# Moving the attention stretches and mixes of batch 1 within FFN block 0, and one stretch of batch 7

## The chip, the cores and the metric

The kernel runs on one core of a Trainium2 chip. The metric is the device time of one execution in microseconds (us). The kernel before takes 837.13 us (median of 3 runs, 836.72 to 837.36).

## The reference

```python
kv = einsum('bhsd,bhse->bhde', k, v)              # 8 batches, 8 heads, 576 rows, 64 columns
out = einsum('bhsd,bhde->bhse', q, kv)
x = out / sqrt(mean(out*out, -1) + 1e-6) * g      # heads side by side: 576 rows of 512
u = x + (x^T @ U @ V)^T                           # U: 576x32, V: 32x576, mixes the rows
y = u + relu(u @ w_ch1) @ w_ch2                   # 512 -> 2048 -> 512
```

Everything is float32; the two weight matrices of the FFN are the large part.

## The kernel before

**Blocks of rows.** The 8 x 576 = 4608 rows of u are cut into nine blocks of 512. Blocks 0 to 2 go through the FFN directly. Blocks 3 to 8 go through it in three stages of two blocks each by a seven-product scheme (P1 to P7), in which one product with a piece of the weights is a unit. Every float32 factor is split into a high and a low float32r part, and a product is three matmuls (high-high, high-low, low-high).

**Block 0.** The FFN runs over 16 chunks f of 128 hidden columns. Chunks 0 to 4 of block 0 are interleaved by hand with the attention of batch 0. From chunk 5 on the loop in `build` runs: two halves of the first product (`ffn1`, six matmuls each), the relu in a high and a low part, two halves of the second product (`ffn2`) of the chunk before. So a chunk has four places behind which other work can be put, numbered 4f to 4f+3: behind the first half of `ffn1`, behind the relu, behind the first half of `ffn2` and behind the second. One such FFN step is six matmuls. Only in block 0 the weights, which arrive as 64-bit words, are also decoded: `decode_w` gives six VectorE and three ScalarE instructions a chunk, issued two chunks ahead (`AHEAD`), and from chunk 10 on a store of the decoded weights on SP's queue (`wf`). Behind each relu GpSimd stores quarters of finished weights (`SPREAD`, `weight_quarters`).

**Attention of the later batches.** Each batch has four pairs of heads. `RUNS` lists (pair, (block or stage, place)). At such a place `run(before, now, after)` issues one stretch for three pairs at once: on TensorE the t-product of the pair before (`t_product`, L387 and L390, x^T U), the kv product of the pair after (`kv_product`, L300) and the out product of the pair now (`out_product`, L319); then, on the other engines, `t4_step` (L400 to L406) splits the t-product into `t4`, `kv_move` (L181) copies kv, `squares` (L329 raw copies, L333 squares), `stats_step` (L348 to L351 and L343 to L345) and `mul_step` (L363) scale x, and `turn_step` (L377) turns it and sends it through DRAM to `ut32` (four stores, L380, and one load, L382). The stretch also starts the next kv and q loads. `MIXES` lists the places of `mix_step`: two matmuls `t4` x V (L463), two additions to `ut32` (L470), and for batch 1 a split into the high and low rows (L422, L423) that the next block's first product reads. The stages' places are numbered by units; there a mix comes in two parts (`mix_part`).

**Order.** TensorE's order is the program order, written by hand. The orders of VectorE, ScalarE and SP's queue come from the scheduler, which prefers what stands earlier in the program among what it holds ready; each engine then runs its list in order.

**Buffers.** `bank()` gives one of two accumulator banks (`pp`); a stretch takes both and so does a mix of a batch up to 2. x has two buffers (`x_sb`), the turned x (`xt`) one, `t4` three, `kv_sb` and `q_sb` one each.

```python
def run(before, now, after):
    one, two = banks()
    if before: t_product(*before, two[:, NT * D:NT * D + P])
    ...
    if now: out_product(*now, (one, two))
    if before: t4_step(*before)
```

Of the kernel before, what the change touches and what calls it, by code (L numbers as in the profile page):

```python
# [37 lines left out]
KEEP = 4  # L38
FROM_DRAM = 5
COMBOS = [(1, f) for f in (1, 2, 4, 5, 7, 8, 10, 11, 13, 14)] + [(2, f) for f in (4, 5, 7, 8, 10, 11)]  # L40
RUNS = [((1, 0), (0, 20)), ((1, 1), (0, 28)), ((1, 2), (0, 37)), ((1, 3), (0, 45)), ((2, 0), (0, 54)),
# [4 lines left out]
MIXES = {(1, 0): ((0, 26),), (1, 1): ((0, 43),), (1, 2): ((0, 51),), (1, 3): ((0, 60),),  # L46
# [46 lines left out]
def build(ctx: ExitStack, tc: tile.TileContext, kv_in, kvt0_in, kvt_in, q_in, uv_in, g_in, w_in, out):  # L93
# [277 lines left out]
    def turn_step(b, p):  # L371

        x = state[b, p]["x"]
        xt = state[b, p].get("xt")
        if xt is None:
            xt = sc.tile([P, 4, NT, 32], F32, name="xt")
        nc.vector.transpose(out=xt.rearrange("p k i j -> p i k j"), in_=x.rearrange("p i (k j) -> p i k j", j=32))  # L377
        xd = xds[p % 2]
        for a in range(4):
            nc.sync.dma_start(out=xd[:, QO[a]:QO[a] + QL[a]].rearrange("(k j) n -> j k n", k=4),  # L380
                              in_=xt[32 * a:32 * a + 32, :, 0:QL[a] // 32].rearrange("p k i j -> p k (i j)"))
        nc.sync.dma_start(out=ut32[p], in_=xd)  # L382
# [154 lines left out]
    def x32_tiles(q):  # L537

        return [once(("x32", q % 2, i), lambda: const.tile([P, 2, 2 * BLK], F32, name="x32", tag=f"u_{2 - 2 * (q % 2) + i}"))
                for i in range(2)]  # L540
# [18 lines left out]
    def factor(q, names, es=slice(0, 2)):  # L559

        x11, x12, x21, x22 = [t[:, es, n * BLK:(n + 1) * BLK] for t in x32_tiles(q) for n in range(2)]
        t = st[:, es]

        def diff(a, b, t=t):
            less(t, a, b)
            return t

        plans = dict(P1=lambda: x11, P3=lambda: x22, P2=lambda: x21, P5=lambda: diff(x12, x11),
                     P6=lambda: diff(x22, t), P4=lambda: diff(x21, t), P7=lambda: diff(x22, x12, kept_t(2)[:, es]))
        for name in names.split():  # L570
            src = plans[name]()
            own = place(name)
            hi, lo = own[:, es, 0], own[:, es, 1]
            nc.scalar.mul(out=hi, in_=src, mul=g_sb)
            nc.vector.scalar_tensor_tensor(out=lo, in0=src, scalar=g_sb, in1=hi.bitcast(F32), op0=ALU.mult, op1=ALU.subtract)  # L575
# [485 lines left out]
    def run(before, now, after):  # L1061

        one, two = banks()
        if before:
            t_product(*before, two[:, NT * D:NT * D + P])
        if after:
            kv = (two if after[0] < NATIVE and after[1] % 2 else one)[:, BLK - D:]
            kv_product(*after, kv)
        if now:
            out_product(*now, (one, two))  # L1070
        if before:
            t4_step(*before)
        if after:
            kv_move(*after, kv)
            following(load_kv, *after)
        if now:
            squares(*now)
            stats_step(*now)
            mul_step(*now)
            following(load_q, *now)  # L1080
            if now not in TURNS:
                turn_step(*now)
# [16 lines left out]
    def at_block(n, what, j=NC - 1):  # L1099
        later.setdefault((None, j, n), []).append(what)  # L1100

    def at(spot, what):
        if spot[0] < NC:
            at_block(spot[1], what, spot[0])
        else:
            at_stage(spot[0] - NC, spot[1], what)
# [3 lines left out]
                         for i, t in enumerate(x32_tiles(0))])  # L1110
    pairs = [pair for pair, _ in RUNS]
    at(RUNS[0][1], lambda: run((1, 0), None, (1, 1)))
    for i, (pair, spot) in enumerate(RUNS[1:], 1):
        at(spot, lambda i=i, pair=pair: run(pairs[i - 1] if i > 1 else None, pair, pairs[i + 1] if i + 2 < len(pairs) else None))
    for pair, spot in TURNS.items():
        at(spot, lambda pair=pair: turn_step(*pair))
    for pair, spots in MIXES.items():
        if pair[0] > 2:
# [4 lines left out]
    for e, pair in enumerate((2, 3)):  # L1123
        at_block(MIXES[4, pair][1][1] + 1, lambda e=e: factor(0, "P1 P5 P6 P4 P2 P7 P3", slice(e, e + 1)))
    for b, spot in CARRY.items():
# [136 lines left out]
```

## Time and profile before

| | |
|---|---|
| median of 3 runs | 837.13 us (836.72 to 837.36) |
| the profiled execution | 837.33 us, of which 835.6 us are the profile's span |
| TensorE matmuls | 820.7 us, 98% of the span |
| TensorE weight loads | 673.2 us, 81% |
| VectorE / ScalarE / GpSimd | 585.4 us (70%) / 443.4 us (53%) / 80.3 us (10%) |
| DMA | 198.39 MB, mean 237 GB/s |

Busy times of matmuls overlap the weight loads (PEld). The timeline lists instructions with their start, duration, engine, line, output and inputs, and in brackets the idle time of the engine ahead of them and what ended it; the duration of a matmul is longer than the distance to the next, since they are pipelined. Times run from the start of the span. Block 0's loop from chunk 6 on lies between 64.79 and 138.58 us, the second Strassen-like stage begins at 517.97 us.

### The profile page before, as it was taken

The numbers are of one execution on the slowest core, as the hardware profiler recorded it, in microseconds if no ns is written. First come the engines' busy times: TensorE is split into PE (matmuls) and PEld (weight loads), VectorE is DVE, ScalarE is ACT, GpSimd is POOL, SyncE is SP. The second block draws the span as 40 slices with busy tenths as digits, with TensorE's granted clock in tenths as the row PEclk, the third lists the DMA queues.
The fourth block names the chain that finished last, engine by engine and source line by source line (L and its number), as shares of the span: only waits on it lengthen the run. The fifth ranks groups of instructions, "written<-read, shape, count | busy, mean of one in ns | idle before, by whom it ended". The sixth has DMA issues, their size and how long they took to land.

```text
span 835.6 us, 14368 instructions
## 1 busy us (share of the span) xinstructions
PE 820.7 (98%) x5492; PEld 673.2 (81%) x5492; DVE 585.4 (70%) x1016; ACT 443.4 (53%) x810; POOL 80.3 (10%) x159
## 2 busy tenths in 40 slices
PE   8999799999999999999999999999999999999998
PEld 7777678888888888888888888788888888888887
DVE  5999885888776678666785688568736943582376
ACT  5978752544443445365645664656346724542462
POOL 3002214244330221000000000000000000000000
PEclk9999999999999999999999999999999999999999
DMA  9984767699887779467777768667555685555554
GB/s 346 415 340 144 225 200 226 219 321 277 262 252 266 239 214 316 160 236 262 241 264 236 264 238 282 231 204 242 178 187 196 207 281 197 182 196 195 202 200 153
DMA packets 66357, 198.39 MB, mean 237 GB/s; under 512 B 8176, under 2 KB 27376, under 8 KB 55536
## 3 DMA queue, kind: packets, MB, share of 16 engines
q1 hardware_dynamic: 57184, 167.97, 58.9%
q0 software_dynamic: 8960, 29.37, 10.5%
q8 instruction: 43, 0.70, 0.3%
q14 instruction: 26, 0.21, 0.1%
q10 hardware_dynamic: 144, 0.13, 0.0%
HBM read 146.84 MB, written 50.59 MB: 236 GB/s over the span
## 4 chain that ended last, share of the span: by engine, by line
PE 83%; DVE 6%; DMA 6%; ACT 3%; issue 1%; SPq 0%; ACTq 0%; DVEq 0%
PE yy L671 25%; PE yy L773 23%; PE y L508 13%; PE h L484 5%; PE h L485 5%; PE h L486 4%; DMA w1raw<-w_in 2%; PE ya L723 2%; DMA out<-x 1%; DMA raw<-w_in 1%; PE pp L300 1%; PE pp L319 1%; DVE dec L164 1%; PE h L300 1%; DVE uc L575 1%
## 5 line engine op out<-in xcount | busy, mean ns | idle before, releaser
L671 PE MATMUL yy<-uc,wt 128*128 128x512 f32 x1008 | 234.1, 391 | 0.9 <-ACT t L405 0.9
L671 PEld LDWEIGHTS yy<-uc,wt 128*128 128x128 f32 x1008 | 188.0, 188 | 40.7 <-ACT t L405 1.3
L773 PE MATMUL yy<-dec,wt 128*128 128x512 f32 x468 | 113.8, 391 | 0.3 <-DVE dec L662 0.3
L508 PE MATMUL y<-hh,ws 128*128 128x512 f32 x336 | 113.4, 393 | 0.0
L773 PE MATMUL yy<-hh,wt 128*128 128x512 f32 x312 | 103.3, 390 | 0.0
L773 PEld LDWEIGHTS yy<-dec,wt 128*128 128x128 f32 x468 | 87.2, 188 | 18.9 <-DVE dec L662 0.7
L662 DVE TENSOR_TENSOR hl<-hk,hh 128x512 fp32r<-128x512 f32 x72 | 48.1, 686 | 39.7 <-ACT hh L701 39.5
L662 DVE TENSOR_TENSOR dec<-hk,dec 128x512 fp32r<-128x512 f32 x72 | 48.9, 686 | 37.1 <-ACT dec L701 36.7
L508 PEld LDWEIGHTS y<-hh,ws 128*128 128x128 f32 x336 | 63.1, 188 | 13.8
L773 PEld LDWEIGHTS yy<-hh,wt 128*128 128x128 f32 x312 | 58.6, 188 | 12.4
L484 PE MATMUL h<-ut,ws 128*128 128x512 f32 x168 | 67.5, 402 | 0.0
L485 PE MATMUL h<-ut,ws 128*128 128x512 f32 x168 | 66.6, 396 | 0.0
L486 PE MATMUL h<-ut,ws 128*128 128x512 f32 x168 | 66.4, 395 | 0.0
L508 PE MATMUL y<-hl,ws 128*128 128x512 f32 x168 | 65.8, 391 | 0.0
L773 PE MATMUL yy<-hl,wt 128*128 128x512 f32 x156 | 60.7, 389 | 0.0
L701 ACT CAST dec<-hk 128x512 fp32r<-128x512 f32 x72 | 44.2, 621 | 29.0 <-PE yy L773 14.9
L701 ACT CAST hh<-hk 128x512 fp32r<-128x512 f32 x72 | 44.0, 622 | 27.0 <-PE yy L773 22.8
L659 ACT COPY sp<-yy 128x1024 f32<-128x1024 f32 x35 | 35.5, 1014 | 32.6 <-PE yy L671 25.3
L496 ACT ACTIVATE hh<-h 128x512 fp32r<-128x512 f32 x48 | 28.4, 591 | 36.8 <-PE h L486 36.6
L684 ACT ACTIVATE hk<-hk 128x1024 f32<-128x1024 f32 x24 | 25.5, 1061 | 36.3 <-DVE hk L683 36.3
L659 ACT COPY yy<-yy 128x1024 f32<-128x1024 f32 x17 | 17.0, 998 | 43.4 <-PE yy L671 40.5
L501 DVE SCALAR_TENSOR_TENSOR hl<-h,hh 128x512 fp32r<-128x512 f32 x48 | 32.7, 682 | 9.4 <-ACT hh L496 9.4
(237 smaller groups left out, 1348.0 us busy)
## 6 DMA issues: line engine op xcount, KB each, us to landing
wt<-wd SPq DMA_DIRECT2D x84, 1024.0 KB, 4.9
kv_sb<-kv_in SPq DMA_DIRECT2D x29, 512.0 KB, 5.9
raw<-w_in SPq DMA_DIRECT2D x14, 1023.6 KB, 14.9
wd<-dec POOLq DMA_DIRECT2D x44, 256.0 KB, 5.7
wd<-ws POOLq DMA_DIRECT2D x42, 256.0 KB, 4.0
q_sb<-q_in SPq DMA_DIRECT2D x29, 288.0 KB, 6.3
ut<-xd SPq DMA_DIRECT2D x28, 288.0 KB, 4.1
out<-x SPq DMA_DIRECT2D x23, 256.0 KB, 4.6
```

The source lines that it names most:

```text
L484: nc.tensor.matmul(h, lhsT=w1s[f][0][:, d, :], rhs=uh[d], start=(n == 0), stop=False)
L485: nc.tensor.matmul(h, lhsT=w1s[f][0][:, d, :], rhs=ul[d], start=False, stop=False)
L486: nc.tensor.matmul(h, lhsT=w1s[f][1][:, d, :], rhs=uh[d], start=False, stop=(n == ND - 1))
L496: last["relu"] = nc.scalar.activation(out=last["hh"], in_=h, func=AF.Relu)
L501: last["low"] = nc.vector.scalar_tensor_tensor(out=hl, in0=h, scalar=0.0, in1=last["hh"].bitcast(F32), op0=ALU.max, op1=ALU.subtract)
L508: nc.tensor.matmul(acc, lhsT=w2s[f][w][:, c, :], rhs=h[:, cols], start=(f == 0 and w == 0 and h is hh), stop=(f == NF - 1 and w == 1))
L659: last["unit"] = nc.scalar.copy(out=pair_bank("P6") if name == "P1" else spare(name), in_=acc)
L662: return nc.vector.tensor_tensor(out=out, in0=a, in1=b, op=ALU.subtract)
L671: nc.tensor.matmul(acc[:, i], lhsT=w[:, ws_, e * P:(e + 1) * P], rhs=u[:, e, us], start=name in ("P1", "P5") and e == 0 and k == 0, stop=e ...
L684: last["unit"] = nc.scalar.activation(out=to, in_=to if other else acc, func=AF.Relu)
L701: last["unit"] = nc.scalar.copy(out=hh, in_=src)
L773: nc.tensor.matmul(acc[:, c], lhsT=w[:, ws_, c * P:(c + 1) * P], rhs=h, start=name in ("P1", "P5") and kk == 0 and i == 0, stop=kk == KEEP ...
```

## The change

Four places of `RUNS`, all four places of batch 1 in `MIXES`, and one more place of `RUNS` get other numbers; no other line differs.

```diff
-RUNS = [((1, 0), (0, 20)), ((1, 1), (0, 28)), ((1, 2), (0, 37)), ((1, 3), (0, 45)), ((2, 0), (0, 54)),
+RUNS = [((1, 0), (0, 20)), ((1, 1), (0, 25)), ((1, 2), (0, 33)), ((1, 3), (0, 41)), ((2, 0), (0, 50)),
...
-        ((6, 3), (3, 72)), ((7, 0), (3, 84)), ((7, 1), (4, 7)), ((7, 2), (4, 18)), ((7, 3), (4, 29)), (None, (4, 40))]
-MIXES = {(1, 0): ((0, 26),), (1, 1): ((0, 43),), (1, 2): ((0, 51),), (1, 3): ((0, 60),),
+        ((6, 3), (3, 72)), ((7, 0), (3, 84)), ((7, 1), (4, 7)), ((7, 2), (4, 20)), ((7, 3), (4, 29)), (None, (4, 40))]
+MIXES = {(1, 0): ((0, 30),), (1, 1): ((0, 45),), (1, 2): ((0, 54),), (1, 3): ((0, 61),),
```

The stretches of (1,1), (1,2), (1,3) and (2,0) in block 0 come three, four, four and four steps sooner; the mixes of (1,0) to (1,3) four, two, three and one step later. The `t4` of a pair is made in the stretch listed behind its own, so that of (1,1) in the stretch of (1,2). In the second of the three stages the stretch of (7,2), which makes the `t4` of (7,1), comes two units later; its mixes, at places 23 and 25, stay.

## Rows read from the trace of the kernel before

**Rows 1.** The page's head and its busy times by engine.

```profile
span 835.6 us, 14368 instructions
PE 820.7 (98%) x5492; PEld 673.2 (81%) x5492; DVE 585.4 (70%) x1016; ACT 443.4 (53%) x810; POOL 80.3 (10%) x159
```

**Rows 2.** TensorE's waits: line, what it waited for; us in total, times, longest.

```profile
PE pp L463 <- DVE t L406: 4.8, 2, 3.4
PE pp L387 <- DVE x L363: 1.2, 1, 1.2
...
PE yy L671 <- ACT t L405: 0.9, 1, 0.9
PE pp L300 <- DVE ut L470: 0.8, 1, 0.8
```

**Rows 3.** Windows: length, busy us (instructions) by engine, granted clock, DMA share, GB/s.

```profile
62.02:117.49 55.47, 50.12 (x388) 40.28 (x387) 48.16 (x85) 42.59 (x66) 9.98 (x16) 0.94 0.60 191
62.02:95.69 33.67, 31.74 (x256) 25.86 (x255) 31.20 (x55) 27.52 (x42) 7.62 (x12) 1.00 0.53 164
64.79:138.58 73.79, 67.04 (x526) 53.91 (x524) 58.47 (x110) 48.27 (x81) 18.41 (x31) 0.95 0.63 196
102.00:103.00 1.00, 1.00 (x4) 0.90 (x5) 1.00 (x4) 1.00 (x2) 1.00 (x2) 0.50 0.49 184
```

**Rows 4.** TensorE's timeline in block 0.

```profile
74.27 0.50 PE L484 MATMUL h<-ut,ws 128*128 128x512 f32 x1
...
89.88 0.50 PE L508 MATMUL y<-hh,ws 128*128 128x512 f32 x1
...
101.78 0.82 PE L463 MATMUL pp<-v,t 128*128 128x288 f32 x2 [3.42 <-DVE t L406]
102.39 0.63 PE L484 MATMUL h<-ut,ws 128*128 128x512 f32 x1
...
107.60 0.43 PE L387 MATMUL pp<-x,uf 128*32 128x128 f32 x8
...
109.53 0.50 PE L508 MATMUL y<-hh,ws 128*128 128x512 f32 x1
```

**Rows 5.** The chain that ended last, in block 0: start, us, what.

```profile
122.65 1.36 PE y L508 x6
...
130.28 2.72 PE y L508 x12
...
134.36 0.26 PE pp L463 x2
```

**Rows 6.** VectorE's timeline: the scaling of x by three stretches, one split.

```profile
87.00 0.82 DVE L363 TENSOR_TENSOR x<-x,half 128x640 f32<-128x640 f32 x1
...
106.27 0.82 DVE L363 TENSOR_TENSOR x<-x,half 128x640 f32<-128x640 f32 x1
...
120.28 0.83 DVE L363 TENSOR_TENSOR x<-x,half 128x640 f32<-128x640 f32 x1
...
136.09 0.68 DVE L423 SCALAR_TENSOR_TENSOR ut<-ut,g_sb,ut 128x448 fp32r<-128x448 f32 x1 [0.74 <-ACT ut L422]
```

**Rows 7.** ScalarE's timeline in block 0.

```profile
95.01 0.44 ACT L329 ACTIVATE x<-pp 128x320 f32<-128x320 f32 x1
97.15 0.74 ACT L333 ACTIVATE xt<-x 128x640 f32<-128x640 f32 x1 [1.71 <-issue]
...
99.92 0.28 ACT L405 CAST t<-two 64x128 fp32r<-64x128 f32 x1
...
116.90 0.44 ACT L329 ACTIVATE x<-pp 128x320 f32<-128x320 f32 x1
```

**Rows 8.** The stage of batch 7's stretches: VectorE's `t4`, TensorE's timeline.

```profile
554.33 0.29 DVE L406 TENSOR_TENSOR t<-two,t 64x128 fp32r<-64x128 f32 x1
...
549.54 7.14 PE L671 MATMUL yy<-uc,wt 128*128 128x512 f32 x30
556.51 0.29 PE L463 MATMUL big<-v,t 128*128 128x288 f32 x1
```

## The prediction, made before the change was run

> **What bounds the kernel now.** I read the page first. TensorE is busy 820.7 of 835.6 us [rows 1]: all that any reordering can win is the remainder and whatever clock is lost. So the list of TensorE's waits is next [rows 2]. The reader is to see that three of its entries, 4.8 for two mixes that wait for their `t4`, 1.2 for a t-product that waits for the scaled `x`, 0.8 for a bank that a mix still holds, make up 6.8 us, and that in all of them the waiting line belongs to the attention stretches or mixes of batch 1 in block 0. Only 0.9 us stands in the Strassen stages, where the other half of the change lies.
>
> Third come the windows of block 0 [rows 3]. From the start of FFN chunk 6 (64.79) to the start of block 1 (138.58) VectorE works 58.47 of 73.79 us. While the weights are still being decoded it is denser: 31.20 of 33.67 us, and 48.16 of 55.47 us over the whole decode. So TensorE waits here, but VectorE is near full, and any time won on TensorE must be matched by VectorE doing the same work in less time.
>
> Fourth, TensorE's timeline [rows 4] gives the price of the longest wait. The mix of pair (1,1) starts at 101.78 after 3.42 us of nothing, and in the window just behind it the granted clock is 0.50 [rows 3], the lower of the two levels (1.2 GHz). The 12 matmuls behind that mix take from 102.39 to 107.60, 5.21 us, where 12 take 2.72 at full clock [rows 5]: 2.49 lost. The mix itself takes 0.61 (101.78 to 102.39) against 0.26: 0.35. Together 2.84 us, which belong to the wait.
>
> The Trainium skill, on the page TensorE: Matmul & The Clock Gate, section What's actually happening, advises to hold the ramp for under 1% of a typical kernel's span and not to model single cold matmuls. By that advice the clock would be left out and the available sum would be the waits alone. The trace disagrees for this change: 2.84 us is under 1% of the span, but it is 30% of what can be won, so I keep it.
>
> Available in block 0: 6.8 + 2.84 = **9.6 us**.
>
> **The change, part by part.** One FFN step (six matmuls) is 1.36 us [rows 5].
>
> *What moves.* Nothing is added or removed. Each moved stretch takes with it about 70 small matmuls of TensorE, ten VectorE and eleven ScalarE instructions, and on SP's queue five transfers that turn x around through DRAM, and the next kv (with its tail) and q loads. Its place decides the order in which the scheduler offers these to VectorE, ScalarE and SP. Four steps are one FFN chunk, so a stretch moved by three or four steps passes one chunk's weight decode on these engines; on SP it passes the stores of decoded weights from chunk 10 on. POOL's stores hang on the relu of their own chunk and are passed by nothing. TensorE's total work is unchanged.
>
> *Mixes later.* The mix of (1,1) stood 6 steps behind the stretch that makes its `t4`, now 12 (33 to 45); of (1,2) 6, now 13; of (1,3) 6, now 11; of (1,0) 6, now 10. The worst need seen is the 6 steps, 8.2 us, and the wait of 3.42 on top: 11.6. Twelve steps give 16.3. So the 4.8 us of waiting for `t4` and the 2.84 us of clock go: cost nothing, covered by four and more spare steps. The 0.8 us wait is a bank one: the mix of (1,0) was followed after two steps (2.72 us) by a stretch that needs both banks, so 3.5 us were needed; now three steps, 4.1 us, follow. It goes too.
>
> *Who waits for the later mixes.* Block 1 reads the rows of pair (1,3) 4.8 us after step 61 (two chunk halves of second product, 2.72; two columns of the first product, 1.36; half a column pair, 0.68). In the trace this mix starts at 134.36 [rows 5] and its last half is written at 136.77 [rows 6]: 2.4 us. Cost nothing; if VectorE were still in decode there, it could be up to half a microsecond.
>
> *What is late next: x.* The t-product of (1,1) now comes 8 steps, 10.9 us, after the products of its pair instead of 9, and that of (1,2) keeps 8, of (1,3) 9 (12.2 us). From the end of a stretch (the start of the next matmul: 74.27, 89.88, 109.53 [rows 4]) to the scaled `x` (starts 87.00, 106.27, 120.28 plus 0.8 [rows 6]) the trace shows 13.6, 17.2 and 11.6 us. Bounds at step 33: 13.6 - 10.9 = 2.7 above, and none below (a gain is excluded, since the wait was 1.2 at most and is counted as won already). At step 41: 17.2 - 10.9 = 6.3 above, 0 below. At step 50: 17.2 - 12.2 = 5.0 above, 0 below. I take 1.0, 1.0 and 0.4, near the lower ends: the nearest row is the 11.6 us chain, the last of the three, and the 13.6 and 17.2 were run behind one more chunk's decode, which the stretches now precede. The 17.2 also holds a time of 1.71 us [rows 7] in which ScalarE could not overwrite the turned `x` of the pair before, whose stores had begun only when TensorE, held up by that same `x`, was already running the next stretch.
>
> *What is late next: banks.* A stretch leaves its two banks when the second raw copy ends: 95.01 + 0.44 - 89.88 = 5.6 us after its end for (1,2), 116.90 + 0.44 - 109.53 = 7.8 for (1,3) [rows 4, 7]. The mix of (1,1) now follows the stretch of (1,3) by four steps, 5.4 us, and so does the mix of (1,2) that of (2,0). Bounds each: 0 and 2.4. I take 0.6 and 0.3, since a late first copy there was a ScalarE idle behind VectorE's decode, and decode is nearly over by then.
>
> *What is late next: decode.* Each stretch now stands before one more decode; the last chunks' weights come that much later and are wanted up to 9.6 us sooner, so that VectorE's work would have 73.79 - 9.6 = 64.2 us. At its dense share of 0.93 it needs 63.1, at the 0.87 of the whole decode 67.2 [rows 3]: bounds 0 and 3.0. I take 0.5, since the 0.87 holds stalls that TensorE's own waits caused.
>
> Sum of new waits: 1.0 + 1.0 + 0.4 + 0.6 + 0.3 + 0.5 = 3.8 us, none alone long enough to be like the 3.42 that brought the low clock. Gain in block 0: 9.6 - 3.8 = **5.8 us**. Check by density: VectorE's 58.47 us must fit in 73.79 - 5.8 = 68.0, a share of 0.86, just under the 0.87 that it has over the whole decode. The gain is kept downstream: behind block 0 the list has almost no waits to refill [rows 2], and the loads that stretches start move with them.
>
> *The stretch of (7,2), two units later.* Its `t4` of (7,1) was ready at 554.62, 5.1 us after TensorE resumed at 549.54, and the mix at 556.51 did not wait [rows 8]. Now only three units, 4.1 us, lie between, and the mix stays where it is. Bounds: 0 (the chain has less in its way after two more units) and 1.0 (same length). I take 0.4. Nothing is won: TensorE had no wait there, and its 0.9 us wait is earlier.
>
> Total: 5.8 - 0.4 = 5.4 us. The profiled execution took 837.33 us and would become 831.9; that execution stands 0.2 above the median of 837.13, and from the median the forecast is **831.7**.
>
> **The rivals.** *A: x stays late (slower).* The chain from products to scaled x stays 13.6 and 17.2 us. Place: the t-products at steps 33 and 41. Price: 2.7 + 6.3 = 9.0, and after a gap of 6.3 us the low clock as now, 2.84: 11.8 against the 9.6 won, with 0.4 for (7,2): 2.6 slower, 839.7. It decides once both excesses pass 6.4 us together with a clock loss. For it: VectorE's density, and that ScalarE's head was stuck 1.71 us with `t4`'s last cast (99.92) behind it [rows 7], so one late transfer holds all. Against: the stretches pass a decode, and waits here give later steps time. The Trainium skill, same page, section Architectural detail, says both engines take their instructions strictly first in, first out; by that rule a moved chain that stalls also stalls the decode now behind it, which is this rival. The trace agrees as far as the 1.71 us goes.
>
> *B: VectorE becomes the bound (same).* It stays as sparse as over the whole stretch, 0.79. 58.47 us at 0.80 need 73.1: 0.7 won, 0.4 given back, 836.8. For it: the chain's many handovers with ScalarE. Against: 0.87 in the decode part, waits included.
>
> *C: the edit does not reach the other engines.* Their order is the scheduler's, not the list's; if it kept the old one, the chains to x would keep their length, and the time would be A's. Counted with A.
>
> **How the numbers follow.** Forecast 0.74, own range 829 to 834. B 0.10, A with C 0.16. About 0.2% (1.7 us) is what a measurement of this kernel tells from no change: faster 0.74, same 0.10, slower 0.16. Low end: waits of 0.5 in all and nothing lost at (7,2), 9.6 - 0.5 = 9.1, 828.0. The high end goes through B and just into A, 838.0; beyond it lie most of A and beneath the low end a little.
>
> **What would show it.** Right: no wait for `t4` in block 0, clock 1.00 in every window from 60 to 140, block 1 starting near 133 instead of 138.6, VectorE's share up to about 0.86, small waits at the t-products of (1,1) and (1,2). Wrong: a gap over 3 us at a t-product or a first product waiting for decoded weights, the clock at 0.50 again, or a wait near 556 of more than 1 us.

## The result, and the profile after

The changed kernel takes **842.59 us** (median of 4 runs, 840.79 to 842.91), the kernel before in the same comparison 837.25 (836.72 to 837.73): a ratio of 1.0060, interval 1.0046 to 1.0074. It is slower by 5.3 us, where 5.4 less were forecast. The profiled execution took 842.45 us, of which 840.6 are the profile's span. The page's head and busy times, as in [rows 1]:

```profile
span 840.6 us, 14365 instructions
PE 822.0 (98%) x5492; PEld 674.7 (80%) x5492; DVE 585.1 (70%) x1016; ACT 443.5 (53%) x810; POOL 82.1 (10%) x159
```

The work is the same on every engine; only its order differs. TensorE's waits (line, what it waited for; us in total, times, longest) answer to [rows 2]:

```profile
PE pp L387 <- DVE x L363: 7.2, 1, 7.2
PE pp L387 <- DVE ut L470: 3.5, 1, 3.5
...
PE big L463 <- DVE t L406: 0.8, 1, 0.8
```

The two waits for `t4` (4.8) and the one for a bank at L300 (0.8) are gone, as forecast. The one for `x` of (1,1) (1.2) is not in the list either, but only because a longer wait at the same t-product covers it (number 5 below). In their place stand two waits at t-products, 10.7 us together. The timeline of TensorE in block 0, with the end of batch 7's stage as its last line, shows where:

```profile
69.07 0.50 PE L508 MATMUL y<-hh,ws 128*128 128x512 f32 x1
...
76.03 0.42 PE L463 MATMUL pp<-v,t 128*128 128x288 f32 x2
...
84.07 0.62 PE L387 MATMUL pp<-x,uf 128*32 128x128 f32 x8 [3.50 <-DVE ut L470]
...
87.34 0.60 PE L508 MATMUL y<-hh,ws 128*128 128x512 f32 x1
...
105.82 0.65 PE L387 MATMUL pp<-x,uf 128*32 128x128 f32 x8 [7.20 <-DVE x L363]
...
113.08 0.39 PE L484 MATMUL h<-ut,ws 128*128 128x512 f32 x1
...
143.38 0.39 PE L484 MATMUL h<-ut,w1s 128*128 128x512 f32 x1
...
561.46 0.37 PE L463 MATMUL big<-v,t 128*128 128x288 f32 x1 [0.82 <-DVE t L406]
```

The first wait is at step 33, in front of the stretch of (1,2); the second at step 41, in front of that of (1,3). Each has a clock loss behind it. The stretch at step 33 takes 84.07 to 87.34 = 3.27 us, where the same stretch takes 1.93 at full clock [rows 4: 107.60 to 109.53]: 1.3 lost. Behind step 41 the stretch and twelve matmuls take 105.82 to 113.08 = 7.26 us, against 1.93 + 2.72 [rows 4, 5]: 2.6 lost. So the new cost is 3.5 + 7.2 + 1.3 + 2.6 = 14.6 us, and the 9.6 of before are no longer there: +5.0. Block 1 begins at 143.38 instead of 138.58, 4.8 later, and the span is 5.0 longer. The windows (columns as in [rows 3]) show the same:

```profile
80.00:90.00 10.00, 6.50 (x86) 5.23 (x85) 8.52 (x19) 5.98 (x8) 3.14 (x4) 0.83 0.50 154
90.00:100.00 10.00, 8.62 (x39) 6.80 (x37) 6.48 (x11) 6.75 (x13) 0.00 (x0) 1.00 0.71 237
100.00:110.00 10.00, 4.18 (x74) 3.70 (x75) 8.63 (x19) 5.86 (x11) 5.36 (x8) 0.56 0.56 160
```

The clock is 0.56 in the last of them, so nearly all of it at the lower level (1.2 GHz), behind 7.2 us in which TensorE did nothing. The middle window matters most: there neither VectorE (6.48) nor ScalarE (6.75) is full, and yet `x` of (1,2) is not ready before 105.68. The two timelines tell why. VectorE, from step 33 to the late `x`:

```profile
81.09 0.82 DVE L363 TENSOR_TENSOR x<-x,half 128x640 f32<-128x640 f32 x1
...
82.43 1.22 DVE L164 SCALAR_TENSOR_TENSOR dec<-raw,top 128x1024 uint32<-128x1024 uint32 x1
83.57 0.45 DVE L470 TENSOR_TENSOR ut<-pp,ut 128x288 f32<-128x288 f32 x1
...
84.69 0.42 DVE L470 TENSOR_TENSOR ut<-pp,ut 128x288 f32<-128x288 f32 x1
...
91.14 1.23 DVE L164 SCALAR_TENSOR_TENSOR dec<-raw,top 128x1024 uint32<-128x1024 uint32 x1 [0.24 <-ACT top L168]
...
96.25 1.23 DVE L164 SCALAR_TENSOR_TENSOR dec<-raw,top 128x1024 uint32<-128x1024 uint32 x1 [1.35 <-ACT top L168]
97.40 0.81 DVE L348 TENSOR_REDUCE sums<-xt 128x10 f32<-128x640 f32 x1
...
104.86 0.82 DVE L363 TENSOR_TENSOR x<-x,half 128x640 f32<-128x640 f32 x1
```

ScalarE, over the same time:

```profile
88.75 1.09 ACT L167 COPY dec<-raw 128x1024 uint8<-128x1024 uint8 x1 [2.46 <-DMA wf<-dec]
...
90.97 0.43 ACT L329 ACTIVATE x<-pp 128x320 f32<-128x320 f32 x1
...
96.08 0.73 ACT L333 ACTIVATE xt<-x 128x640 f32<-128x640 f32 x1
...
99.44 1.09 ACT L167 COPY dec<-raw 128x1024 uint8<-128x1024 uint8 x1 [2.43 <-DMA wf<-dec]
...
101.85 0.30 ACT L349 ACTIVATE ta<-sums,eps 128x10 f32<-128x10 f32 x1
```

Follow the chain of (1,2) from the end of its stretch at 87.34. Its raw copy L329 stands behind L167, a decode step that could not overwrite its `dec` buffer (there are two) before the store of the chunk two before had landed (2.46 us of waiting). The square L333 is at 96.08. VectorE's sum L348 is at 97.40, right behind a decode step of 1.23. Then ScalarE's next step L349 waits until 101.85, behind another L167 that stood 2.43 us for a store. L363 ends at 105.68. From the stretch's end to `x`: 18.3 us, where the forecast hoped for far less than before's 17.2. SP's queue, from the same time, shows the store's side (start, us to issue):

```profile
83.68 0.59 SPq L270 DMA_DIRECT2D wf<-dec  x1
84.84 4.42 SPq L380 DMA_DIRECT2D xd<-xt  x4
...
92.15 0.33 SPq L382 DMA_DIRECT2D ut<-xd  x1
...
92.99 5.03 SPq L270 DMA_DIRECT2D wf<-dec  x2
```

The stretch that now comes sooner puts the turning of `x` of (1,1) behind one store of decoded weights, where two stood ahead of it before. But the place in the queue is a small part of ScalarE's two waits. The first store left at 83.68, as soon as its data were written (L164 from 82.43 to 83.65), and landed 5.0 us later. The second left at 92.99, 0.6 us after its data (L164 from 91.14 to 92.37), and landed 6.4 us later. The kernel before has four such stores up to 102 us, and they landed 3.1 to 4.0 us after they left. So it is the time to land that held ScalarE; why it was longer here, no run shows.

### The profile page after: what moved, and what is told of

Same layout as the page of the kernel before. It is cut to its first block, busy times and chain, and to the rows that moved or that the text cites. A ratio compares the mean times of both kernels' runs of the same rounds, so it can differ in the third digit from the quotient of the medians.

```text
span 840.6 us, 14365 instructions
## 1 busy us (share of the span) xinstructions
PE 822.0 (98%) x5492; PEld 674.7 (80%) x5492; DVE 585.1 (70%) x1016; ACT 443.5 (53%) x810; POOL 82.1 (10%) x159
## 4 chain that ended last, share of the span: by engine, by line
PE 81%; DMA 8%; DVE 7%; ACT 3%; issue 1%; SPq 0%; POOL 0%; ACTq 0%; DVEq 0%
PE yy L671 26%; PE yy L773 24%; PE y L508 11%; PE h L484 4%; PE h L485 4%; PE h L486 4%; DMA kv_sb<-kv_in 2%; PE ya L723 2%; DMA raw<-w_in 1%; DMA wf<-dec 1%; PE pp L300 1%; DVE uc L575 1%; PE pp L319 1%; DMA wd<-dec 1%; DMA w2raw<-w_in 1%
## 5 line engine op out<-in xcount | busy, mean ns | idle before, releaser
L671 PE MATMUL yy<-uc,wt 128*128 128x512 f32 x1008 | 233.8, 390 | 0.0
L671 PEld LDWEIGHTS yy<-uc,wt 128*128 128x128 f32 x1008 | 188.0, 188 | 39.4
L484 PE MATMUL h<-ut,ws 128*128 128x512 f32 x168 | 66.4, 395 | 0.1
L485 PE MATMUL h<-ut,ws 128*128 128x512 f32 x168 | 65.6, 390 | 0.0
L486 PE MATMUL h<-ut,ws 128*128 128x512 f32 x168 | 65.4, 389 | 0.0
```

What stands on the lines that cost most here:

```text
L484: nc.tensor.matmul(h, lhsT=w1s[f][0][:, d, :], rhs=uh[d], start=(n == 0), stop=False)
L485: nc.tensor.matmul(h, lhsT=w1s[f][0][:, d, :], rhs=ul[d], start=False, stop=False)
L486: nc.tensor.matmul(h, lhsT=w1s[f][1][:, d, :], rhs=uh[d], start=False, stop=(n == ND - 1))
L671: nc.tensor.matmul(acc[:, i], lhsT=w[:, ws_, e * P:(e + 1) * P], rhs=u[:, e, us], start=name in ("P1", "P5") and e == 0 and k == 0, stop=e ...
```

## The experiments

A yardstick for them all: **block 0's length**, from the first kv matmul (L300) of the stretch of (1,0) to block 1's first product. Before: 59.69 to 138.58, **78.9 us**. After: 59.71 to 143.38, **83.7 us**. Ratios are against the kernel before, measured in the same comparison.

**1. Block 0's part alone**

```diff
-        ... ((7, 2), (4, 20)) ...
+        ... ((7, 2), (4, 18)) ...
```

> The block 0 part of the change alone; the stretch of (7,2) is back at unit 18. Theory: the loss is block 0's, two waits of 3.5 and 7.2 us at the t-products of (1,1) and (1,2) with the half clock behind them; so about 5 us slower than before, 841.8 to 842.6, the 0.8 us wait at the mix of (7,1) gone. Rival: the stage of batch 7 carries a part of the loss, then 841 or less.

840.68 us, ratio 1.0058 (1.0040 to 1.0075). Taken as a time this lies in the rival's span (841 or less), but the kernel before ran at 836.65 in this comparison, 0.6 lower. The ratio is that of the whole change (1.0060): within the intervals, the loss is in block 0. TensorE's waits in this run:

```profile
PE pp L387 <- DVE x L363: 4.6, 1, 4.6
PE pp L387 <- DVE ut L470: 3.5, 1, 3.5
...
PE yy L671 <- ACT t L405: 0.7, 1, 0.7
```

The wait for `x` is 4.6 here instead of 7.2, with the same code in block 0 (82.1 us long): ScalarE's waits for stores were 2.92 and 0.30 instead of 2.46 and 2.43. So part of the wait hangs on when a store lands.

**2. The stretch of (7,2) alone**

```diff
-        ... ((7, 2), (4, 18)) ...
+        ... ((7, 2), (4, 20)) ...
```

(from the kernel before)

> The move of the stretch of (7,2) by two units alone. Theory: the mix of (7,1) waits 0.8 us for its t4 as in the changed kernel, and the 0.9 us wait of before at the unit behind the stretch of (7,1) stays, since it is earlier: 837.9 to 838.2, 0.8 us slower. Rival: the move took that 0.9 us wait away (it is missing from the changed kernel's list), then 837.0 to 837.3.

837.13 us against 836.65, ratio 1.0011 (0.9999 to 1.0022): between nothing and 0.2%. The time lies in the rival's span, but with the kernel before 0.6 lower here it does not tell the two apart. The wait of 0.9 us at L671 is 0.5 in this run, and the profile has the new wait, as the changed kernel's has:

```profile
PE big L463 <- DVE t L406: 0.8, 1, 0.8
```

**3. The mix of (1,0) back at its old place**

```diff
-MIXES = {(1, 0): ((0, 30),), ...
+MIXES = {(1, 0): ((0, 26),), ...
```

> The changed kernel with the mix of (1,0) back at step 26; the rest as changed. Theory A, the bank: the t-product at step 33 waits 3.5 us because the mix of (1,0) was put four steps later and its additions stand behind more decode in VectorE's list; with the mix at 26 the wait falls to 1.3 us or less (x was written 1.3 us after TensorE came) and the time to about 839. Theory B, the full list: VectorE has that much work ahead of step 33 whatever the order; the wait moves to the scaled x, stays 3 to 5 us, and the time stays at 842 to 843.

847.16 us, ratio 1.0143 (1.0114 to 1.0172), slower still, and outside both expectations. The place is now one step behind the stretch at 25, and the mix finds both banks taken; the wait moves there:

```profile
77.62 0.93 PE L463 MATMUL pp<-v,t 128*128 128x288 f32 x2 [4.29 <-ACT x L329]
```

At step 33 nothing waits; TensorE waits for `x` at two later t-products, 5.1 and 3.2 us (the profiled execution took 851.99 us, the other three 846.6 to 847.6). This does not tell the theories about `x` apart, but it shows the bank at work: a stretch keeps both until its raw copies (L329) are done, and the mix waits 4.29 us for them.

**4. No stores of decoded weights in block 0** (the changed kernel; the stores and the loads that bring them back are left out)

```diff
-FROM_DRAM = 5
+FROM_DRAM = 8
...
-BACK = {(2, 3): ((0, 5), (1, 5), (0, 6), (1, 6)), (2, 6): ((0, 7),), (2, 7): ((1, 7),)}
+BACK = {}
```

> The changed kernel without the stores of decoded weights in block 0 and their loads in block 2; block 2 adds the two halves of those weights again on VectorE (12 additions of 0.7 us). Theory A, ScalarE's head: the 7.2 us wait at the t-product of (1,2) holds two waits of ScalarE, 2.46 and 2.43 us, for those stores to leave the decode buffer, with the copies and statistics of x queued behind; without them the wait falls to 2 to 3 us, less clock is lost, and the time is 835 to 838. Theory B, VectorE's list: the chain waits for decode work in both lists; the wait stays above 5 us and the time at 840 to 843.

840.80 us, ratio 1.0054 (1.0038 to 1.0071). Block 0 is 79.5 us, 4.1 shorter, but ahead of it 0.7 and behind it 1.6 us are lost, so the total moves little. The wait at step 33 stays 3.5; those for `x` are 3.00 at step 41 and 1.09 at step 50, in place of 7.2:

```profile
84.76 0.43 PE L387 MATMUL pp<-x,uf 128*32 128x128 f32 x8 [3.50 <-DVE ut L470]
...
102.34 0.66 PE L387 MATMUL pp<-x,uf 128*32 128x128 f32 x8 [3.00 <-DVE x L363]
...
119.59 0.43 PE L387 MATMUL pp<-x,uf 128*32 128x128 f32 x8 [1.09 <-DVE x L363]
```

The wait is as theory A has it, the time as theory B. The chain of (1,2) still takes 14.5 us, from 87.74 to 102.19. The stores are a part of the lateness, not the whole of it.

**5. The mix of (1,0) out of the way**

```diff
-MIXES = {(1, 0): ((0, 30),), ...
+MIXES = {(1, 0): ((0, 58),), ...
```

> The changed kernel with the mix of (1,0) put at step 58, between the last two mixes, so that it holds no bank between the stretches of (1,1) and (2,0). Theory A, the bank: the 3.5 us wait at step 33 was for the two banks that this mix held; now only x is waited for, 1.5 us or less, no half clock there, and the time falls by 2 to 5 us against the changed kernel, to 837.5 to 840.5. Theory B, the full list: VectorE is that far behind at this point anyway, x comes 3 us or more late, and the time stays at 841 to 843.

840.31 us, ratio 1.0044 (1.0027 to 1.0061), near to theory A; block 0 81.7 us. TensorE's timeline at steps 33 and 41:

```profile
82.26 0.43 PE L387 MATMUL pp<-x,uf 128*32 128x128 f32 x8 [1.78 <-DVE x L363]
...
103.57 0.66 PE L387 MATMUL pp<-x,uf 128*32 128x128 f32 x8 [7.37 <-DVE x L363]
```

Of the 3.50 at step 33, 1.7 belonged to the bank that this mix held; 1.8 would have been waited for `x` of (1,1) anyhow. Behind the 1.78 the low clock does not follow: it is 1.00 in every window from 82 to 92 us. The wait at step 41 is as long as ever.

**6. Before's stretches, its mixes later**

```diff
-MIXES = {(1, 0): ((0, 26),), (1, 1): ((0, 43),), (1, 2): ((0, 51),), (1, 3): ((0, 60),),
+MIXES = {(1, 0): ((0, 26),), (1, 1): ((0, 49),), (1, 2): ((0, 59),), (1, 3): ((0, 62),),
```

> The kernel before with its stretches where they were and three mixes later: (1,1) at 49, (1,2) at 59, (1,3) at 62, each behind the next stretch. Theory: the 4.8 us of waiting for t4 and the half clock behind it (2.8 us) are the mixes' doing alone and go; new are a bank wait of 0 to 2.4 us at step 49, four steps behind the stretch of (1,3), and an earlier x wait: 830.5 to 834 against 836.7 to 837.3 of before. Rival: VectorE and ScalarE are the bound and the waits come back at the t-products: 836 to 839.

836.41 us, ratio 0.9998 (0.9988 to 1.0007): no change, as the rival has it. The waits for `t4` are gone, and the time is waited a little later, at step 45, for `x` of (1,2):

```profile
105.60 0.65 PE L387 MATMUL pp<-x,uf 128*32 128x128 f32 x8 [5.34 <-DVE x L363]
```

So the `t4` waits of before covered a second lateness. `x` of (1,2) is ready at 102 to 109 us in every kernel up to here, wherever its stretch and the mixes stand.

**7. The kernel before without the stores** (left out as in 4)

```diff
-FROM_DRAM = 5
+FROM_DRAM = 8
...
+BACK = {}
```

> The kernel before without the stores of decoded weights in block 0, as in the run without them on the changed kernel, which lost about 1.8 us behind block 0. Theory A: ScalarE's waits for the stores (4.2 us) and the late turned x (1.7 us) hold up the t4 of (1,1); its wait falls from 3.4 to under 1.5 us and the half clock is gone: block 0 shorter by 3 to 5 us, 834 to 836. Theory B: decode work alone sets it; block 0 unchanged within 1 us, 837 to 839.

837.13 us, ratio 1.0006 (0.9997 to 1.0016), block 0 78.1. That is theory B. The waits for `t4` are 5.1 in all instead of 4.8. In the old order the stores cost block 0 at most 0.8 us; what holds the chains there is not they.

**8. No decode of chunks 10 to 15** (the changed kernel; the last six chunks' weights are a constant from GpSimd, ScalarE still makes the high copy and the stores stay)

```diff
 def decode_w(f):
     tmp = dec.tile([P, 2 * DM], F32, name="dec")
     t = tmp.rearrange("p (w c) -> p w c", w=2)
...
+    if f >= 10:
+        raws.pop(f)
+        def copy_only():
+            nc.gpsimd.memset(tmp, 0.01)
+            w = weight_slot(f"ws{f}", [P, 2, 2, DM], F32R, f)
+            nc.scalar.copy(out=w[:, 0], in_=t)
+            nc.gpsimd.memset(w[:, 1].bitcast(F32), 0.0)
...
+        return dict(H=copy_only)
```

> The changed kernel without the decode of the weight chunks 10 to 15 (their weights are left out: GpSimd fills them with a constant, ScalarE still makes the high copy; the six stores to wf stay, taken from the finished chunk). Theory L (the chain of the stretch at step 33 takes 14 to 19 us because steps of the weight decode stand between its hops in VectorE's and ScalarE's lists): in block 1, where nothing is decoded, the same chain takes some 9 us from the stretch's first matmul to the end of L363 (batch 2's: copies at 168.11, L363 done at 175.2), so here x of (1,2) is done before 98 us and TensorE's waits for x at steps 41 and 50 are gone, at most 0.5 us together; block 0 some 7 to 10 us shorter than the changed kernel's 83.7 us. The wait of 3.5 for L470 at step 33 stays at 1 to 3.5, as chunks up to 9 are decoded as before. Rival H (the chain's own handovers and the banks make it long, decode or not): the chain of (1,2) stays at 13 us or more and the waits for x at 2 us or more.

834.11 us, ratio 0.9978 (0.9963 to 0.9994), as theory L has it. The wait for `x` of (1,2) is gone, and none stands at step 50; the bank wait at step 33, behind chunks that are decoded as ever, is 2.7. Block 0 runs from 60.55 to 134.31, 73.8 us: 9.9 shorter than the changed kernel. Its lines are numbered 15 higher (L378 is L363). ScalarE and VectorE run the chain of (1,2) behind a stretch that ends at 86.79, where TensorE's next second product starts:

```profile
86.79 0.79 PE L523 MATMUL y<-hh,ws 128*128 128x512 f32 x1
```

```profile
88.26 0.44 ACT L344 ACTIVATE x<-pp 128x320 f32<-128x320 f32 x1
...
91.25 0.74 ACT L348 ACTIVATE xt<-x 128x640 f32<-128x640 f32 x1 [0.23 <-DMA xd<-xt]
92.88 0.30 ACT L364 ACTIVATE ta<-sums,eps 128x10 f32<-128x10 f32 x1 [0.89 <-DVE sums L363]
```

```profile
92.03 0.82 DVE L363 TENSOR_REDUCE sums<-xt 128x10 f32<-128x640 f32 x1 [0.69 <-ACT xt L348]
...
94.15 0.82 DVE L378 TENSOR_TENSOR x<-x,half 128x640 f32<-128x640 f32 x1
```

From 86.79 to 94.97: 8.2 us, against 18.3. The chain's own steps and handovers take 8; the other 10 are decode steps, and the stores they wait for, in the two lists. So the decode with its stores makes `x` late. The run takes the work out and does not reorder it: that the order of the two lists counts, and not the sheer amount of work, is argued from the idle time. VectorE is busy 12.59 and ScalarE 12.52 of the 18.3 us of the changed kernel's chain. No run keeps the decode and only moves it out of the chain's way.

**9 and 10. The other way: later stretches behind a known late `x`** (from the kernel before)

```diff
-... ((1, 1), (0, 28)), ((1, 2), (0, 37)), ((1, 3), (0, 45)), ((2, 0), (0, 54)),
+... ((1, 1), (0, 28)), ((1, 2), (0, 37)), ((1, 3), (0, 49)), ((2, 0), (0, 57)),
...
-MIXES = {(1, 0): ((0, 26),), (1, 1): ((0, 43),), (1, 2): ((0, 51),), (1, 3): ((0, 60),),
+MIXES = {(1, 0): ((0, 26),), (1, 1): ((0, 46),), (1, 2): ((0, 60),), (1, 3): ((0, 62),),
```

> From the kernel before: only the stretch of (1,3) goes from step 45 to 49 and that of (2,0) from 54 to 57, the mixes of batch 1 to 26, 46, 60 and 62. Theory X (x of (1,2) is ready at 101 to 107 us wherever its stretch stands, so the next stretch belongs behind that time, and a mix into the gap in front of it): step 49 comes at 107 to 108 us, so no wait for x at it; the t4 waits of 4.8 and 3.4 us are at most 1 us; block 0 some 6 to 9 us shorter than before's 78.9, time 829 to 833. Rival: the later stretches push x of (1,3) and the last mix into the end of block 0, a wait of 2 to 5 us for x at step 57 or for t4 at block 1's start: 834 to 838.

**833.08 us**, ratio **0.9955** (0.9939 to 0.9972): faster than both kernels, and at the upper end of what was expected. Block 0 is 59.05 to 133.01, 74.0 us, in a profiled execution of 831.72 us, the shortest of the six. The wait for `x` of (1,2) and both for `t4` are gone; at step 49 only 0.4 is left, for a bank:

```profile
103.11 0.42 PE L463 MATMUL pp<-v,t 128*128 128x288 f32 x2
...
108.08 0.43 PE L387 MATMUL pp<-x,uf 128*32 128x128 f32 x8 [0.43 <-DVE ut L470]
```

Block 0 is 4.9 us shorter than before's, where 6 to 9 were expected: small waits of 0.8 remain (for `hl`, for a bank, and at step 57, which the profile puts down to `hh`, though `x` of (1,3) was written only 0.15 us ahead of it), and 1.2 for `x` of (1,1). Number 10 has the stretches at 38, 50 and 58 and the mix of (1,1) at 47:

> As the run before it, with the stretches of (1,2), (1,3) and (2,0) a step later each (38, 50, 58) and the mix of (1,1) at 47. Theory X: x of (1,1) is no longer waited for either (1.2 us before), the rest as in the run before it: 829 to 832. Rival: what is late at the end of block 0 (x of (1,3) at step 58, t4 of (1,3) at step 62) is a step later too: 834 to 838.

834.87 us, ratio 0.9982 (0.9972 to 0.9993), block 0 75.8 us: the rival's time, but not for the rival's reason. The 1.2 is gone, but `x` of (1,2) comes later too, at 110.00, and is waited for again: 1.93 us at step 50, with the clock at 0.50 from 111 to 114 us behind it. One step too far takes back over half of the gain.

**11. The changed kernel with only its third stretch and what follows later**

```diff
-... ((1, 3), (0, 41)), ((2, 0), (0, 50)),
+... ((1, 3), (0, 49)), ((2, 0), (0, 57)),
...
-... (1, 2): ((0, 54),), (1, 3): ((0, 61),),
+... (1, 2): ((0, 60),), (1, 3): ((0, 62),),
```

> The changed kernel with only its third stretch and what follows it put later: (1,3) at 49 instead of 41, (2,0) at 57 instead of 50, the mixes of (1,2) and (1,3) at 60 and 62; the stretches of (1,1) and (1,2) stay three and four steps sooner, the mixes of (1,0) and (1,1) at 30 and 45. Theory X (one step of the change costs, the t-product at step 41, which comes before x of (1,2) is ready at 105 us): step 49 comes at some 109 us, the wait of 7.2 us and its half clock are gone, the wait of 3.5 us at step 33 stays with 1.4 us of half clock; block 0 76 to 78 us, time 834.5 to 838. Rival (sooner stretches of (1,1) and (1,2) push decode behind them, which comes back as a wait elsewhere): a new wait of over 3 us at step 49 or at a first product, time 839 or more.

838.15 us, ratio 1.0021 (1.0008 to 1.0033), just outside the expected span; block 0 59.51 to 138.15, 78.6 us, 5.0 shorter than the changed kernel. The 7.2 is gone and the 3.5 has stayed, but a new wait stands at a second product:

```profile
100.82 0.71 PE L508 MATMUL y<-hh,ws 128*128 128x512 f32 x1 [2.43 <-ACT hh L496]
```

and ScalarE's timeline shows what it waited for:

```profile
99.18 1.09 ACT L167 COPY dec<-raw 128x1024 uint8<-128x1024 uint8 x1 [3.15 <-DMA wf<-dec]
100.18 0.59 ACT L496 ACTIVATE hh<-h 128x512 fp32r<-128x512 f32 x1
```

The relu `hh` that TensorE needs stands in ScalarE's list behind a decode step that stands for a store. In the changed kernel this fell into the wait for `x`. So both readings hold a part: step 41 was the dear one, and the sooner stretches of (1,1) and (1,2) also push stores and decode back. Number 9 has the same later part but for the mix of (1,1), at 46 for 45; against it the sooner first stretches, with the mix of (1,0) behind them, cost 78.6 - 74.0 = 4.6 us.

**12. Both mixes in the gap**

```diff
-... ((1, 3), (0, 49)), ((2, 0), (0, 57)),
+... ((1, 3), (0, 48)), ((2, 0), (0, 57)),
...
-MIXES = {(1, 0): ((0, 30),), (1, 1): ((0, 45),),
+MIXES = {(1, 0): ((0, 40),), (1, 1): ((0, 44),),
```

(from number 11)

> As the run before it, with (1,3) at 48 and the mixes of (1,0) and (1,1) at 40 and 44, both in the gap between the stretches at 33 and 48. If the wait at step 33 is for banks that the mix at 30 holds, it falls from 3.5 to 1.8 us (then for x of (1,1), as with this mix at 58), and nothing else appears: block 0 75 to 77, time 833.5 to 836.5. Rival: two mixes four steps apart hold each other's banks, a wait of 1 to 4 us at one of them or at step 48: 837 or more.

837.24 us, ratio 1.0012 (1.0002 to 1.0021), block 0 76.9. At step 33 the 3.5 falls to 1.8, now for `x`, as expected, and neither mix takes the other's banks. But the wait for `hh` stays (2.0, with 0.9 for `hl` and some low clock behind it). Block 0 is in the expected span; the time is above it, since the profile has 2.3 us more behind block 0 than the kernel before, 1.1 of them at a mix that waits for its `t4` at 286.00. Why that one waits stays open. Sooner first stretches do not pay in any arrangement tried.

## Why the prediction was wrong

**What bounds the kernel: right, with one error.** The 9.6 us of waits and clock were there, and none of them stands in the changed kernel's list, though the 1.2 for `x` of (1,1) is covered and not removed. The error is to call them available. Number 6 removed the same waits for `t4` and got nothing: right behind them stood `x` of (1,2). A wait on the path hides the next late thing, and its length is an upper bound of a gain.

**"The mixes later": right.** No mix of batch 1 waits for `t4`, and block 1 does not wait for the mix at 61. The margin was smaller than "four and more spare steps": ten to thirteen steps of 1.36 us against 11.6 leave 1.5 to 4.5.

**"What is late next: x", step 41: the step that failed.** The chain of 17.2 us was to shorten, as "the 13.6 and 17.2 were run behind one more chunk's decode, which the stretches now precede", and 1.0 us was taken between bounds of 0 and 6.3. It did not shorten: 18.3 us, a wait of 7.2, above the upper bound, and 2.6 of clock. A stretch that comes sooner does not pass a chunk's decode as a block. Its ten VectorE and eleven ScalarE steps are woven between decode steps, and at a handover between the two engines it may meet one more, as L329 and L349 did behind L167. `x` of (1,1) came 5.9 us sooner for three steps (81.91 against 87.82 [rows 6]); that of (1,2) only 1.4 sooner for four (105.68 against 107.09). Number 8 measures the share: 8.2 us of chain, 10 of decode with its stores. The nearest row was the 17.2 of the same pair in the same decode, and the prediction chose the 11.6 of a pair that ran when decode was nearly over. The other two terms for `x` were about right: 1.0 taken at step 33, where number 5 shows 1.8 once the bank is out of the way, and 0.4 at step 50, where the changed kernel does not wait.

**The bank at step 33: failed too.** The 0.8 us "goes too", it said, since three steps, 4.1 us, follow the mix where 3.5 were needed. The need was taken from a place where VectorE came to the additions soon. Here the mix's matmuls are at 76.03, and its first addition, which the t-product waited for, ends at 84.02, 8.0 us later, behind `x` of (1,1) and decode steps. Number 5 shows that it is the bank: 1.7 of the 3.5, and the clock behind it.

**Banks at 45 and 54 (0.6 and 0.3), decode (0.5):** no bank wait stands there. The decode term had the right place and the wrong form: not weights that arrive late, but a relu behind a decode step (number 11).

**The check by density was no check.** VectorE's 58.47 us would have fitted. In the window of 90 to 100 us VectorE and ScalarE are both two thirds busy and the chain still crawls, so neither engine's capacity sets its length; what is left is the order of the two lists and the stores that L167 waits for.

**"None alone long enough to be like the 3.42 that brought the low clock": failed**, since both new waits did, 3.9 us of the 14.6.

**The stretch of (7,2):** 0.4 taken; the profile shows a wait of 0.8 at the mix, and the time of number 2 allows 0 to 1.8 us. Right within what can be told.

**The rivals.** A had the side and the second place: a wait for `x` at step 41 with the low clock behind it. It forecast 839.7, from 2.7 + 6.3 of waits and 2.84 of clock; the chip gave 10.7 and 3.9. At step 33 stood a bank, which A did not name, over 1.8 us for `x` (number 5). C is excluded in its plain form: the other engines' lists did change, as (1,1) shows. B is excluded: the loss is a wait, with VectorE at 62.9 of 83.7 us, as busy as before's 62.9 of 78.9. The row that spoke for A, ScalarE's head held up with a chain behind it, was the one to follow. The Trainium skill's statement that both engines work strictly first in, first out (TensorE: Matmul & The Clock Gate, section Architectural detail) agrees with the 2.43 us for which L349 and the relu stood behind L167.

## What to carry to other kernels

When a chain hops between two engines that also work through something long, its length is set by what stands between its hops in both lists, so starting it sooner may gain little (1.4 us for four steps); place its consumer behind the time at which it is really ready, and put other work into the gap (number 9: 0.45% where the change lost 0.6%). Before a removed wait is counted as won, look for what becomes ready next behind it in the trace, and test it by removing that wait alone. Ask of each buffer how long its reader took to come at this place, not at a quiet one.

## What the runs showed of the hardware

In the changed kernel a gap of 7.2 us on TensorE cost another 2.6 us at the lower clock behind it, and one of 3.5 us 1.3. How long a gap is does not by itself tell its price: one of 1.78 us (number 5) cost nothing, with the granted clock at 1.00 behind it, and one of 1.93 us (number 10) brought it to 0.50 and made the stretch behind it 2.82 us long instead of 1.93. A single store of decoded weights (512 KB), which took 3.1 to 4.0 us to land in the kernel before and 5.0 and 6.4 at the two waits of the changed one, held ScalarE's head for 2.4 us each time (3.15 in number 11, where it took 6.6), and with it relus and square roots that have nothing to do with the store. In the changed order, removing all the stores shortened block 0 by 4.1 us; in the old order, by 0.8 and the total by nothing: the same transfers were nearly free or not by what stood behind them.
